# An adaLN block with a spectral filter and a SwiGLU FFN: the order of its loads, its statistics and its inverse transform is changed

## The chip, the cores and the metric

The kernel runs on one core of one Trainium2 chip. The metric is the device time of one execution in microseconds (us). A NeuronCore has five engines that run beside each other and wait for one another through semaphores: TensorE (matmuls; the profile calls it PE, and its weight loads PEld), VectorE (DVE), ScalarE (ACT), GpSimd (POOL) and SyncE (SP, which here only issues DMAs). Each engine works through its own list of instructions in order. Matmuls write to PSUM, a small memory from which only VectorE and ScalarE read here; everything else lies in SBUF, whose first dimension is 128 partitions.

## What is computed

```python
sa, ca, ga, sb, cb, gb = split(silu(c) @ w_mod, 6)          # c: (1, 640), w_mod: (640, 3840)
h = layernorm(x) * (1 + ca) + sa                            # x: (1, 2048, 640)
y = irfft2(rfft2(h) * (w_r + 1j * w_i))                     # over both axes, weights (2048, 321)
x = x + ga * y
h = layernorm(x) * (1 + cb) + sb
g = silu(h @ w_gate)                                        # (640, 1728)
u = h @ w_up
out = x + gb * ((g * u) @ w_down)                           # (1728, 640)
```

Inputs and output are bf16. `rfft2` and `irfft2` are the real two-dimensional Fourier transform over tokens and features and its inverse.

## The kernel before

All work is done with matmuls against constant tables. The 2048 tokens are 16 tiles of 128, `x_sb[:, t]` (token 16 p + t is on partition p). The code is one long list of calls; the order of the calls in the text is the order in each engine's list, since the scheduling is manual. Dependences between tiles become semaphore waits. A tile pool hands out its buffers by tag; a new tile of a tag waits until the old one in that buffer is read. Loads from HBM are DMAs that SP issues in the order of the text (lines 190 to 220 and a few later ones); two of them, the second half of `Wa`, are issued by ScalarE from within its own list (step `W0`, line 206).

**First stage, LN1 and the first transform over tokens (lines 265 to 358).** Per tile t: `ln1_stats` (L269 to L271, VectorE: two `bn_stats` and an aggregate) or, for the tiles in `ON_ACT`, `ln1_act` on ScalarE (a sum, then a sum of squares); `means` (L285, L288) writes the negated mean; `root` (L247, L323, ScalarE) the square root; `ready` takes the reciprocal (L328, VectorE) and calls `scaled`, which multiplies a 128x128 table with 1/std (`Fs`, L295, GpSimd for most tiles, VectorE for the first and last); `turn` (L303, L306, TensorE) multiplies the tile with `Fs` into a PSUM tile `tp`; `turned` (L312, ScalarE, VectorE for the last two) copies it to `hT`. `mod_ca` computes the column form of 1 + ca: 25 small matmuls (L239, into `mpsA`), then an addition on VectorE (`one_p_ca`, L341). `rs` multiplies it into the table `Rp` (L334). The string `plan` (L354) writes out by hand the order in which all these steps are issued: a letter for the step, a number for the tile. In it `a0`, the whole of `mod_ca`, stands after `t5` and before `s9`.

**Second stage, the filter (lines 379 to 508).** The frequencies along the tokens are in 16 groups g. Per group, in the order `order` = 1..10, 0, 11..15: `dfwd` (L383) transforms along the features into `zps`; `zcopy` (L393, ScalarE); `over_t` (L413 to L429) finishes the token transform into `xps`; `xcopy` (L434); `product` (L441, VectorE) multiplies with the weights; `sums` (L448 to L461, VectorE); `over_t_back` (L470 to L474, TensorE), three groups later, into `vps`; `vcopy` (L477, ScalarE) into `V2`. A group has 128 frequencies, one per partition. In `_freqs` (L45) they stand in two halves: slot 0 (32 j + g) on partitions 0 to 63, slot 1 (32 j + 32 - g) on partitions 64 to 127. The weights lie likewise: `Wa` holds groups 0 to 7 and `Wb` groups 8 to 15, and each is loaded in halves of 64 partitions, `slot0` (L202) and `slot1` (L206; rows in reverse, 642 bytes each). `swap(h)` exchanges two columns of a weight tile on VectorE.

**The last products back (lines 515 to 538).** The last four groups' `over_t_back` come after all other work of the filter. Between them stand `gate_rows` for ga (L253, 10 matmuls into `ga_ps`), `mod_cols` for cb and sb (L239, 50 small matmuls into `c_ps`) with two ScalarE operations that read them (L527, L528), two blocks of `keep_warm` (L260, 8 matmuls of constants each), and the DMAs of the gate and down weights `Wg` and `Wd_sb` (L530, L531). `Wg` goes into the buffer of `wm_g`, which the `c_ps` matmuls read. Then VectorE multiplies ga into the table `Rinv_sb` (L536).

**Head of LN2 (lines 641 to 665).** `dinv(t)` (L621, 6 matmuls, then a ScalarE copy `W2`, L624) transforms back along the features; `over_p(t)` (L630, 2 matmuls) finishes the token transform, and VectorE adds the result to `x_sb` in place (L636), or ScalarE copies it and `add_y` adds it (L633, L639) for tiles in `BY_ACT`. Seven `dinv` and four `over_p` run here. For tiles 0 and 1 follow `ln2_stats` (L551 to L553), the root on ScalarE, `ln2_xn` (L578: (x - mean) / std on VectorE into `xn2`), a transpose on TensorE (L591, `tp`) and the affine 1 + cb, sb (L599 VectorE, L601 ScalarE) into `h2Ta`.

**FFN (lines 671 to 735).** The tokens go in five chunks of 2, 4, 4, 4 and 2 tiles (`CHUNKS`); sc is the chunk. Per chunk: `gu13` (L678, the last 64 columns of gate and up together), then 13 rounds fc: ten matmuls into `gu` (L701), silu on ScalarE (`sg`, L704), the product on VectorE into `AT` (L705). Then per tile two halves of 14 down matmuls (L732, `oo`), the addition of x (L734) and the store (L735). Beside the rounds of a chunk VectorE prepares the next one: `ln2_stats` in rounds 1 to 4, `ln2_newton` (L560 to L569, round 5: 1/std by three Newton steps from an integer guess, all on VectorE), `ln2_xn` in rounds 6 and 7, then a DMA transpose (L582) and the affine (L607, L610). L707 multiplies the last 64 columns in round 2.

In chunk 0 more is done. `gate_rows` for gb (L253, `gb_ps`) comes after `gu13`; ten of the 14 row blocks of `Wd_sb` are multiplied with it on GpSimd (L692, the "folds"), the other four on VectorE (L711) in rounds 8 to 11. And round fc runs `over_p(4 + fc)` and `dinv(7 + fc)` ahead of its matmuls, so that all 16 tiles are added to x by round 11. In PSUM `dinv`, `over_p` and the down matmuls share one tag `oo` with two buffers; `gu`, `gu13`, `tp` and the first four `over_p` share `vv` with two.

Of the kernel before, what the change touches and what calls it, by code (L numbers as in the profile page):

```python
# [17 lines left out]
NT, P = 16, 128  # L18
# [106 lines left out]
def adaln_block_kernel(  # L125
# [82 lines left out]
    slot0(0)
    for i in range(2):
        nc.sync.dma_start(Ws[0][64:128, i, 0], w_rows[i][1][:, 0])  # L210
    nc.sync.dma_start(wm_sa[:], wm_v[:, :, 0:D])
    nc.sync.dma_start(Mf[:, 4:8], M_dram[:, 4:8])
    nc.sync.dma_start(Mi[:, 0:8], Mi_dram[:, 0:8])
    slot0(1)
    slot1(nc.sync, 1)
    nc.sync.dma_start(Mf[:, 8:16], M_dram[:, 8:16])
# [45 lines left out]
    with tc.tile_pool(name="ph2", bufs=2) as ph2, \  # L262
# [46 lines left out]
        def turned(t):  # L309
            tp = tps.pop(t)  # L310
            copy = nc.vector.tensor_copy if t >= NT - 2 else nc.scalar.copy
            copy(hT[:, :, :, t, :], tp[:, 0:NC5, :].rearrange("p c (g j) -> p c g j", j=8))  # L312
# [22 lines left out]

        ON_ACT = (1, 8)

        def mod_ca():
            mps = ps1.tile([P, NC5], F32, name="mpsA", tag="xps", bufs=1)
            mod_cols(mps, wm_ca, 0, True)  # L340
            nc.vector.tensor_scalar_add(one_p_ca[:], mps[:], 1.0)  # L341

# [7 lines left out]
            "g": lambda t: nc.gpsimd.tensor_copy(sc_rep[:], sc_col[:].unsqueeze(2).to_broadcast([P, NC5, 128])),  # L350
            "W": lambda t: slot1(nc.scalar, t), "a": lambda t: mod_ca(), "x": lambda t: rs(3 * t, 3 * t + 1, 3 * t + 2),
# [84 lines left out]
        def product(g, PP):  # L436

            X = Xs.pop(g)
            for h in range(2):
                w = Ws[g // 8][:, :, g % 8, 0:LH] if h == 0 else Ws[g // 8][:, :, g % 8, 320:320 - LH:-1]  # L440
                nc.vector.tensor_tensor(PP[:, :, :, LH * h:LH * h + LH], X[:, :, LH * h:LH * h + LH].unsqueeze(1).to_broadcast([P, 2, 2, LH]),  # L441
                                        w.unsqueeze(2).to_broadcast([P, 2, 2, LH]), ALU.mult)
# [72 lines left out]
        for n in range(NGR - 1 - LAG, NGR):  # L515
            if n == 14:
                c_ps = ps1.tile([P, 2, 512], F32, name="c_ps", tag="xps", bufs=1)
                for j, w_ in enumerate((wm_g[:, :, D:2 * D], wm_sb)):
                    mod_cols(c_ps[:, j, 0:NC5], w_, 0)
# [6 lines left out]
            if n == 14:  # L526
                nc.scalar.add(one_p_cb[:], c_ps[:, 0, 0:NC5], 1.0)  # L527
                nc.scalar.copy(modcols[:, 2, :], c_ps[:, 1, 0:NC5])  # L528
                Wg = big.tile([P, NC5, FFM], BF16, name="Wg", tag="wg")
                nc.sync.dma_start(Wg[:], B_w_gate[:, 0:FFM].rearrange("(c5 dp) f -> dp c5 f", dp=P))  # L530
                nc.sync.dma_start(Wd_sb[:, 0:13, :], B_w_down[0:FFM, :].rearrange("(fc fp) d -> fp fc d", fp=P))  # L531
                nc.gpsimd.memset(Wd_sb[64:128, 13, :], 0.0)
                nc.sync.dma_start(Wd_sb[0:64, 13, :], B_w_down[FFM:FF, :])
                keep_warm(ps1, "xps", 1, 8)
# [3 lines left out]
        keep_warm(ps1, "xps", 1, 8)  # L538

# [77 lines left out]
    def dinv(t):  # L617
        o = ps3.tile([P, 2, 512], F32, name="oo", tag="oo")
        for odd, blocks in enumerate(((0, 3, 4), (2, 1, 4))):
# [6 lines left out]
    def over_p(t, tag="vv"):  # L626
        W2 = W2s.pop(t)
        y = ps3.tile([P, 2, 512], F32, name="yy", tag=tag)
        for odd in range(2):
# [10 lines left out]

    BY_ACT = (1, 2, 3)
    ybs = {}
    dinv(0)
    dinv(1)
    over_p(0)
    ln2_stats(0)
    dinv(2)
    over_p(1)
    add_y(1)
# [5 lines left out]
    ln2_xn(0, 1)  # L655
    over_p(2)
    dinv(4)
    dinv(5)
    tp = ln2_turn_pe()
    add_y(2)  # L660
    dinv(6)
    nc.scalar.activation(warm[:], rstd2[:, 1:2], ACT.Silu)
    ln2_affine_pe(tp)
    over_p(3)
    add_y(3)
    AT2 = [big.tile([P, NFC, 512], BF16, name=n, tag=g) for n, g in (("ATa", "w"), ("ATb", "mi"))]
# [4 lines left out]
    for sc, (c0, c1) in enumerate(CHUNKS):  # L671
# [14 lines left out]
        if sc == 0:  # L686

            gb_ps = ps3.tile([P, 2, 512], F32, name="gb_ps", tag="oo")
            gate_rows(gb_ps, wm_gb, False)
            nc.scalar.copy(g_bc[1][:].rearrange("p (o h) -> p o h", o=2), gb_ps[:, :, 0:320])  # L690
            for f in range(10):
                nc.gpsimd.tensor_tensor(Wd_sb[:, f, :], Wd_sb[:, f, :], g_bc[1][:], ALU.mult)  # L692
        for fc in range(NFC - 1):
            if sc == 0 and fc < 12:
                over_p(4 + fc, "oo")
            if sc == 0 and fc < 9:
                dinv(7 + fc)
            gu = ps3.tile([P, 2, 512], F32, name="gu", tag="vv")
# [6 lines left out]
            nc.vector.tensor_tensor(AT[:, fc, :C], gu[:, 1, :C], sg[:, :C], ALU.mult)  # L705
            if fc == 2:
                nc.vector.tensor_tensor(AT[0:64, 13, :C], u13b[:, :C], sg13[:, :C], ALU.mult)  # L707
# [4 lines left out]
            if sc + 1 < len(CHUNKS):  # L712
                m0, m1 = CHUNKS[sc + 1]
                if 1 <= fc < 1 + m1 - m0:
                    ln2_stats(m0 + fc - 1)
                if fc == 5:
                    ln2_newton(sc + 1)
                if fc in (6, 7):
                    for t in range(m0 + 2 * (fc - 6), min(m1, m0 + 2 * (fc - 6) + 2)):
                        ln2_xn(sc + 1, t)  # L720
                if fc == 7:
                    ln2_turn(sc + 1)
        if sc + 1 < len(CHUNKS):
            ln2_affine(sc + 1, range(NC5))
        for tl in range(n):
# [3 lines left out]
            for h in range(2):  # L729
                oo = ps3.tile([P, 2, 512], F32, name="oo", tag="oo")  # L730
                for fc in range(NFC):
# [52 lines left out]
```

## Time and profile before

| | us |
|---|---|
| three runs: median (lowest to highest) | 286.33 (285.9 to 286.36) |
| the profiled execution | 286.61 |
| its span, first to last instruction | 284.8 |
| TensorE busy (share of the span) | 263.7 (93%) |
| VectorE busy | 157.1 (55%) |
| ScalarE busy | 110.6 (39%) |
| GpSimd busy | 28.7 (10%) |
| HBM read and written | 21.53 and 2.62 MB |

The profile is that of one execution. It has a page with totals, and views that answer questions: the chain of work that ended last (followed back from the last instruction, at each step to what released it), busy time in stretches of the span, waits (who stood still for whom: total, times, longest), groups of instructions by source line, and a timeline. In a group, `xN` is the count and the durations are those of one instruction; a matmul's duration includes its way through the array, so dense matmuls overlap, and the time of a run of matmuls is read from the chain or the timeline. `PEclk` is the clock granted to TensorE as a share of the full one. The column DMA is the mean busy share of the 16 DMA engines.

### The profile page before, as it was taken

The numbers are of one execution on the slowest core, as the hardware profiler recorded it, in microseconds if no ns is written. First come the engines' busy times: TensorE is split into PE (matmuls) and PEld (weight loads), VectorE is DVE, ScalarE is ACT, GpSimd is POOL, SyncE is SP. The second block draws the span as 40 slices with busy tenths as digits, with TensorE's granted clock in tenths as the row PEclk, the third lists the DMA queues.
The fourth block names the chain that finished last, engine by engine and source line by source line (L and its number), as shares of the span: only waits on it lengthen the run. The fifth ranks groups of instructions, "written<-read, shape, count | busy, mean of one in ns | idle before, by whom it ended". The sixth has DMA issues, their size and how long they took to land.

```text
span 284.8 us, 4821 instructions
## 1 busy us (share of the span) xinstructions
PE 263.7 (93%) x1926; PEld 174.0 (61%) x1926; DVE 157.1 (55%) x440; ACT 110.6 (39%) x198; POOL 28.7 (10%) x47
## 2 busy tenths in 40 slices
PE   5767999999858988999999999999999999999995
PEld 4555787787635766864445764444774444678873
DVE  4678499789251888924863323883421762422432
ACT  7655787785575434412223003322203222202320
POOL 5552000010003960000000000000000000000000
PEclk9979999999997999999999999999999999999999
DMA  6999999005991000410031011004011002011001
GB/s 221 395 223 348 208 382 323 2 2 165 370 371 38 0 2 1 92 48 10 0 59 37 23 48 32 0 5 90 23 46 35 0 0 46 3 47 53 0 2 46
DMA packets 24905, 27.02 MB, mean 95 GB/s; under 512 B 11313, under 2 KB 21938, under 8 KB 24754
## 3 DMA queue, kind: packets, MB, share of 16 engines
q1 hardware_dynamic: 23808, 26.07, 29.9%
q10 hardware_dynamic: 1074, 0.64, 1.3%
q8 instruction: 15, 0.25, 0.4%
q14 instruction: 8, 0.07, 0.1%
HBM read 21.53 MB, written 2.62 MB: 85 GB/s over the span
## 4 chain that ended last, share of the span: by engine, by line
PE 83%; DVE 9%; ACT 3%; DMA 1%; issue 1%; POOL 0%; SPq 0%; DVEq 0%; ACTq 0%; POOLq 0%
PE gu L701 38%; PE oo L732 21%; PE zps L383 4%; PE oo L621 3%; PE xps L424 2%; PE xps L429 2%; PE tp L303 2%; PE tp L306 2%; PE gu L678 2%; DMA x_sb<-in_A_x_dram 1%; DVE x_sb L636 1%; PE vps L470 1%; PE vps L471 1%; PE gb_ps L253 1%; DVE st L270 1%
## 5 line engine op out<-in xcount | busy, mean ns | idle before, releaser
L704 ACT ACTIVATE sg<-gu 128x512 f32<-128x512 f32 (+1 forms) x65 | 33.2, 511 | 75.3 <-PE gu L701 71.2
L701 PEld LDWEIGHTS <-Wg 128*128 128x128 bf16 x325 | 31.7, 98 | 25.5 <-issue 0.7
L701 PEld LDWEIGHTS <-Wu 128*128 128x128 bf16 x325 | 31.8, 98 | 24.5
L734 DVE TENSOR_TENSOR xo<-oo,x_sb 128x320 bf16<-128x320 f32 x32 | 15.7, 491 | 38.6 <-PE oo L732 38.5
L701 PE MATMUL gu<-h2Ta,Wu 128*128 128x256 bf16 (+1 forms) x195 | 34.6, 308 | 0.0
L701 PE MATMUL gu<-h2Ta,Wg 128*128 128x256 bf16 (+1 forms) x195 | 34.6, 308 | 0.0
L705 DVE TENSOR_TENSOR ATa<-gu,sg 128x256 bf16<-128x256 f32 (+1 forms) x39 | 19.9, 509 | 26.5 <-ACT sg L704 26.4
L705 DVE TENSOR_TENSOR ATb<-gu,sg 128x512 bf16<-128x512 f32 x26 | 17.9, 687 | 28.6 <-ACT sg L704 28.5
L701 PE MATMUL gu<-h2Tb,Wu 128*128 128x512 bf16 x130 | 32.3, 379 | 0.0
L701 PE MATMUL gu<-h2Tb,Wg 128*128 128x512 bf16 x130 | 32.3, 379 | 0.0
L732 PE MATMUL oo<-Wd_sb,ATa 128*128 128x320 bf16 x224 | 30.9, 299 | 0.0
L732 PE MATMUL oo<-Wd_sb,ATb 128*128 128x320 bf16 x224 | 30.8, 299 | 0.0
L732 PEld LDWEIGHTS <-ATb 128*128 128x128 bf16 x224 | 21.8, 98 | 8.9
L732 PEld LDWEIGHTS <-ATa 128*128 128x128 bf16 x224 | 21.9, 98 | 8.6
L681 ACT ACTIVATE sg<-gu 64x512 f32<-64x512 f32 (+1 forms) x5 | 2.5, 505 | 49.8 <-PE gu L678 49.7
L621 PE MATMUL oo<-Rinv_sb,V 128*128 128x320 bf16 x96 | 15.4, 299 | 3.3 <-DVE x_sb L636 2.7
L383 PE MATMUL zps<-Rs,hT 128*128 128x324 bf16 x96 | 15.9, 300 | 0.9 <-DVE wtmp L371 0.9
L624 ACT CAST W<-oo 128x640 bf16<-128x640 f32 x16 | 11.0, 694 | 12.6 <-PE oo L621 12.6
L636 DVE TENSOR_TENSOR x_sb<-yy,x_sb 128x640 bf16<-128x640 f32 x13 | 11.1, 854 | 8.1 <-PE yy L630 8.1
L692 POOL TENSOR_TENSOR Wd_sb<-Wd_sb,gb_bc 128x640 bf16<-128x640 bf16 x10 | 13.8, 1415 | 16.8 <-ACT gb_bc L690 16.8
L303 PE MATMUL tp<-Fs,mh 128*128 128x512 bf16 (+1 forms) x32 | 9.5, 391 | 5.5 <-POOL Fs L295 3.9
L621 PEld LDWEIGHTS <-V 128*128 128x128 bf16 x96 | 9.3, 98 | 8.1 <-issue 4.0
(140 smaller groups left out, 333.1 us busy)
## 6 DMA issues: line engine op xcount, KB each, us to landing
out_dram<-xo SPq DMA_DIRECT2D x16, 160.0 KB, 1.8
Wu<-in_B_w_up_dram SPq DMA_DIRECT2D x1, 2080.0 KB, 9.5
Wg<-in_B_w_gate_dram SPq DMA_DIRECT2D x1, 2080.0 KB, 12.6
Wd_sb<-in_B_w_down_dram SPq DMA_DIRECT2D x1, 2080.0 KB, 17.8
wm_g<-in_w_mod_dram SPq DMA_DIRECT2D x2, 800.0 KB, 15.0
Mi<-tab_Mi SPq DMA_DIRECT2D x2, 768.0 KB, 11.6
x_sb<-in_A_x_dram SPq DMA_DIRECT2D x2, 640.0 KB, 9.2
Mf<-tab_M SPq DMA_DIRECT2D x2, 512.0 KB, 9.9
```

Source lines behind the costliest of these rows:

```text
L303: nc.tensor.matmul(tp[:, lo:lo + n, :], lhsT=mh.to_broadcast([P, 128]), rhs=Fs[:].unsqueeze(1).to_broadcast([P, n, 128]), start=True, stop ...
L306: nc.tensor.matmul(tp[:, c5, :], lhsT=block(x_sb[:, t, :], c5), rhs=Fs[:], start=False, stop=(c5 >= 3))
L383: nc.tensor.matmul(zss[g][:, r, :L], lhsT=hT[:, 2 * r + i, g, :, :].rearrange("p t j -> p (t j)"), rhs=Rs[:, 3 * r + i, :], start=(i == 0) ...
L621: nc.tensor.matmul(o[:, odd, 0:320], lhsT=V2[:, b, t, :, :].rearrange("p g j -> p (g j)"), rhs=Rinv_sb[:, odd, i, :], start=(i == 0), stop ...
L624: nc.scalar.copy(W2s[t][:], o[:, :, 0:320])
L636: nc.vector.tensor_tensor(x1t, y[:, :, 0:320], x1t, ALU.add)
L692: nc.gpsimd.tensor_tensor(Wd_sb[:, f, :], Wd_sb[:, f, :], g_bc[1][:], ALU.mult)
L701: nc.tensor.matmul(gu[:, j, :C], lhsT=w_[:, c5, fc * 128:(fc + 1) * 128], rhs=h2T[:, 0:n, c5, :], start=(c5 == 0), stop=(c5 == NC5 - 1))
L704: nc.scalar.activation(sg[:, :C], gu[:, 0, :C], ACT.Silu)
L705: nc.vector.tensor_tensor(AT[:, fc, :C], gu[:, 1, :C], sg[:, :C], ALU.mult)
L732: nc.tensor.matmul(oo[:, 0, 0:320], lhsT=AT[:, fc, tok], rhs=Wd_sb[:, fc, h * 320:(h + 1) * 320], start=(fc == 0), stop=(fc == NFC - 1))
L734: nc.vector.tensor_tensor(xo[:, h * 320:(h + 1) * 320], oo[:, 0, 0:320], x1[:, t, h * 320:(h + 1) * 320], ALU.add)
```

## The change

There are five groups of edits.

1. **Frequency slots.** The two slots of a group alternate over the partitions (slot 0 on even, slot 1 on odd ones) instead of taking a half each; the tables follow from `_freqs`. `Wa` now holds groups 1 to 8, `Wb` groups 9 to 15 and 0. All weight loads are issued by SP, each to every second partition; there are four more small ones, for group 0. `Mf[4:8]` is issued ahead of `wm_sa`.
2. **Scale weights read later.** `mod_ca` is split: `a0`, the matmuls, stands after `R11`, and `a1`, the addition, after `r13`. The plan is otherwise reordered at its start (tile 1 on VectorE, tile 2 on ScalarE), and only the last `turned` is on VectorE.
3. **Products back without stops.** The last four `over_t_back` and `vcopy` follow each other with only `gate_rows` for ga between. Only the `mod_cols` of cb follow, then the DMAs of `Wg` and `Wd_sb`. Both `keep_warm` blocks are gone. `mod_cols` of sb and `gate_rows` of gb move to the head of LN2, ahead of the transpose of tiles 0 and 1.
4. **Newton on GpSimd.** The guess stays on VectorE (three instructions), a product with -0.5 and the three steps, four instructions each, go to GpSimd, one round earlier. Of the ten folds on GpSimd four stay at the start of chunk 0, six follow the Newton steps in round 4. L707's product in chunk 0 moves from round 2 to round 10.
5. **Six tiles of x in the second chunk.** The head of LN2 runs `dinv(0)` to `dinv(4)` and `over_p(0)`, `over_p(1)`; chunk 0 runs `over_p(2)` to `over_p(9)` and `dinv(5)` to `dinv(9)`; `dinv(10)` to `dinv(15)` run in even rounds and `over_p(10)` to `over_p(15)` in odd rounds of chunk 1. The silu table load of ScalarE comes after the affine and `dinv(4)`. `oo` becomes two tags of one buffer each: `ob` for `dinv` from tile 4 on, `oa` for `over_p` in the FFN; the down matmuls alternate between them.

```diff
-    k = np.zeros((NGR, 2, 64), dtype=np.int64)
+    k = np.zeros((NGR, 64, 2), dtype=np.int64)
...
-        k[g, 0] = 32 * np.arange(64) + g
-        k[g, 1] = 32 * np.arange(64) + (32 - g if g else 16)
+        k[g, :, 0] = 32 * np.arange(64) + g
+        k[g, :, 1] = 32 * np.arange(64) + (32 - g if g else 16)
...
+    def filter_rows(h):
+        n = 8 - h
+        for i in range(2):
+            nc.sync.dma_start(Ws[h][1::2, i, 0:n], w_rows[i][1][:, 15 - 8 * h:(7 if h == 0 else 0):-1])
+        for i in range(2):
+            nc.sync.dma_start(Ws[h][0::2, i, 0:n], w_rows[i][0][:, 1 + 8 * h:1 + 8 * h + n])
+        if h == 1:
+            for s_ in range(2):
+                for i in range(2):
+                    nc.sync.dma_start(Ws[1][s_::2, i, 7], w_rows[i][s_][:, 0])
...
-        ON_ACT = (1, 8)
+        ON_ACT = (2, 8)
...
+        def mod_ca(step):
+            if step == 0:
+                mps.append(ps1.tile([P, NC5], F32, name="mpsA", tag="xps", bufs=1))
+                mod_cols(mps[0], wm_ca, 0, True)
+            else:
+                nc.vector.tensor_scalar_add(one_p_ca[:], mps[0][:], 1.0)
...
-        plan = """s0 m0 r0 c0 g0 s2 p1 q1 m1 r1 y0 t0 s3 M2 R2 s4 y1 e0 t1 Y2 s5 M4 R4 p8 W0 e1 t2 t3 s6 Y4 e2 s7 M6 R6
-                  e3 q8 m8 r8 t4 t5 a0 s9 Y6 e4 s10 M9 R9 e5 t6 t7 s11 y8 Y9 e6 e7 t8 s12 M11 R11 e8 t9 s13 m13 r13 t10 Y11
-                  e9 e10 t11 s14 m14 r14 y13 t12 e11 s15 m15 r15 e12 t13 y14 e13 t14 x0 y15 t15 e14 x1 k8 e15"""
+        plan = """s0 m0 r0 c0 g0 s1 m1 r1 y0 t0 p2 q2 m2 r2 s3 m3 r3 y1 t1 e0 s4 y2 y3 t2 e1 s5 M4 R4 s6 t3 e2 Y4 p8 s7
+                  M6 R6 e3 t4 t5 q8 m8 r8 s9 Y6 e4 s10 M9 R9 e5 t6 t7 s11 y8 Y9 e6 e7 t8 s12 M11 R11 a0 e8 t9 s13 m13 r13
+                  a1 t10 Y11 e9 e10 t11 s14 m14 r14 y13 t12 e11 s15 m15 r15 e12 t13 y14 e13 t14 x0 y15 t15 e14 x1 k8
+                  e15"""
...
+        hv = ph4.tile([P, n], F32, name="rs_hv")
+        nc.gpsimd.tensor_scalar_mul(hv[:], v[:], -0.5)
...
-            nc.vector.tensor_tensor(tt[:], y, y, ALU.mult)
-            nc.vector.scalar_tensor_tensor(tt[:], tt[:], -0.5, v[:], ALU.mult, ALU.mult)
-            nc.vector.scalar_tensor_tensor(rstd2[:, g] if it == 2 else y, tt[:], 1.5, y, ALU.add, ALU.mult)
+            nc.gpsimd.tensor_tensor(tt[:], y, y, ALU.mult)
+            nc.gpsimd.tensor_tensor(tt[:], tt[:], hv[:], ALU.mult)
+            nc.gpsimd.tensor_scalar_add(tt[:], tt[:], 1.5)
+            nc.gpsimd.tensor_tensor(rstd2[:, g] if it == 2 else y, tt[:], y, ALU.mult)
...
-            for f in range(10):
+            for f in range(4):
                 nc.gpsimd.tensor_tensor(Wd_sb[:, f, :], Wd_sb[:, f, :], g_bc[1][:], ALU.mult)
...
-            if sc == 0 and fc < 12:
-                over_p(4 + fc, "oo")
-            if sc == 0 and fc < 9:
-                dinv(7 + fc)
+            if sc == 0 and fc < 8:
+                over_p(2 + fc, "oa")
+            if sc == 0 and fc < 5:
+                dinv(5 + fc)
+            if sc == 1 and fc % 2 == 0 and fc < 12:
+                dinv(10 + fc // 2)
+            if sc == 1 and fc % 2 == 1 and fc < 12:
+                over_p(10 + fc // 2, "oa")
...
-            if fc == 2:
+            if fc == (10 if sc == 0 else 2):
                 nc.vector.tensor_tensor(AT[0:64, 13, :C], u13b[:, :C], sg13[:, :C], ALU.mult)
...
-                if fc == 5:
+                if fc == m1 - m0:
                     ln2_newton(sc + 1)
+                    for f in range(4, 10) if sc == 0 else ():
+                        nc.gpsimd.tensor_tensor(Wd_sb[:, f, :], Wd_sb[:, f, :], g_bc[1][:], ALU.mult)
```

More of the change, by code (lines that the diff above doesn't have):

```diff
@@ L334, in rs @@
                 nc.vector.tensor_scalar_mul(Rs[:, i, :], Rp[:, i, :], one_p_ca[:, (i if i < 3 else i - 1):(i if i < 3 else i - 1) + 1])
-        ON_ACT = (1, 8)
[L338 to L341, printed above, removed]
+        ON_ACT = (2, 8)
+        mps = []
+        def mod_ca(step):
[4 more added lines that the diff above has]
+                nc.vector.tensor_scalar_add(one_p_ca[:], mps[0][:], 1.0)
         steps = {
@@ L515, in adaln_block_kernel @@
         for n in range(NGR - 1 - LAG, NGR):
[L516 to L519, printed above, removed]
             over_t_back(order[n], ("vps", "zps")[n % 2])
@@ L525, in adaln_block_kernel @@
                 nc.scalar.copy(g_bc[0][:].rearrange("p (o h) -> p o h", o=2), ga_ps[:, :, 0:320])
[L526 to L534, printed above, removed]
+        c_ps = ps1.tile([P, 2, 512], F32, name="c_ps", tag="xps", bufs=1)
+        mod_cols(c_ps[:, 0, 0:NC5], wm_g[:, :, D:2 * D], 0)
+        Wg = big.tile([P, NC5, FFM], BF16, name="Wg", tag="wg")
+        nc.sync.dma_start(Wg[:], B_w_gate[:, 0:FFM].rearrange("(c5 dp) f -> dp c5 f", dp=P))
+        nc.sync.dma_start(Wd_sb[:, 0:13, :], B_w_down[0:FFM, :].rearrange("(fc fp) d -> fp fc d", fp=P))
+        nc.gpsimd.memset(Wd_sb[64:128, 13, :], 0.0)
+        nc.sync.dma_start(Wd_sb[0:64, 13, :], B_w_down[FFM:FF, :])
+        nc.scalar.add(one_p_cb[:], c_ps[:, 0, 0:NC5], 1.0)
         for odd in range(2):
@@ L627, in over_p @@
         W2 = W2s.pop(t)
-        y = ps3.tile([P, 2, 512], F32, name="yy", tag=tag)
+        y = ps3.tile([P, 2, 512], F32, name="yy", tag=tag, bufs=2 if tag == "vv" else 1)
         for odd in range(2):
@@ L639, in add_y @@
         nc.vector.tensor_tensor(x1[:, t, :], ybs.pop(t)[:], x1[:, t, :], ALU.add)
-    BY_ACT = (1, 2, 3)
+    BY_ACT = (1,)
+    T_IN_FFN = 4
     ybs = {}
@@ L646, in adaln_block_kernel @@
     ln2_stats(0)
+    over_p(1)
     dinv(2)
-    over_p(1)
     add_y(1)
@@ L655, in adaln_block_kernel @@
     ln2_xn(0, 1)
-    over_p(2)
+    c_ps = ps3.tile([P, 2, 512], F32, name="c_ps", tag="oa", bufs=1)
+    mod_cols(c_ps[:, 0, 0:NC5], wm_sb, 0)
+    nc.scalar.copy(modcols[:, 2, :], c_ps[:, 0, 0:NC5])
+    gb_ps = ps3.tile([P, 2, 512], F32, name="gb_ps", tag="ob", bufs=1)
+    gate_rows(gb_ps, wm_gb, False)
+    tp = ln2_turn_pe()
+    nc.scalar.copy(g_bc[1][:].rearrange("p (o h) -> p o h", o=2), gb_ps[:, :, 0:320])
+    ln2_affine_pe(tp)
     dinv(4)
[L658 to L661, printed above, removed]
     nc.scalar.activation(warm[:], rstd2[:, 1:2], ACT.Silu)
-    ln2_affine_pe(tp)
-    over_p(3)
-    add_y(3)
     AT2 = [big.tile([P, NFC, 512], BF16, name=n, tag=g) for n, g in (("ATa", "w"), ("ATb", "mi"))]
@@ L729, in adaln_block_kernel @@
             for h in range(2):
-                oo = ps3.tile([P, 2, 512], F32, name="oo", tag="oo")
+                oo = ps3.tile([P, 2, 512], F32, name="oo", tag=("oa", "ob")[h], bufs=1)
                 for fc in range(NFC):
```

26 lines of the change are left out of this document (8 added, 18 removed).

## The prediction

> **What bounds the kernel now.** I read the chain of work that ended last first, then a table of busy time by stage, then the waits. The chain's shares by engine, and some of its pieces (start us, us, what):
>
> ```profile
> PE 83%; DVE 9%; ACT 3%; DMA 1%; issue 1%; POOL 0%; SPq 0%; DVEq 0%; ACTq 0%; POOLq 0%
> ```
>
> ```profile
> 14.95 0.62 PE mpsA L239 x25
> ...
> 83.62 1.28 ACT L662
> 85.12 0.92 ACT h2Ta L601 x2
> 86.08 0.80 PE gu L678 x5
> 86.87 2.68 PE gb_ps L253 x10
> ...
> 126.99 28.17 PE gu L701 x130
> 155.16 15.21 PE oo L732 x112
> ```
>
> TensorE carries the end. From 118.31 us on it is dense: 130 gate/up matmuls are one piece of 28.17, 112 down matmuls one of 15.21. What is taken off other engines there is worth nothing, and what is added to TensorE there costs its full time. The stages that I use (span cut at first `zps`, first `oo` of `dinv`, first `gu13`, first down matmul):
>
> ```profile
> 0.00:27.86 27.86, 18.96 (x178) 14.50 (x179) 18.79 (x72) 17.64 (x38) 13.28 (x34) 0.94 0.97 298
> 27.86:73.79 45.93, 44.03 (x477) 35.38 (x478) 35.44 (x119) 33.11 (x52) 1.61 (x3) 1.00 0.63 193
> 73.79:86.08 12.29, 8.05 (x61) 5.37 (x61) 5.97 (x15) 8.74 (x15) 0.00 (x0) 1.00 1.05 361
> 86.08:118.31 32.23, 29.31 (x225) 22.55 (x225) 23.84 (x57) 12.97 (x25) 13.76 (x10) 0.95 0.12 24
> 118.31:284.80 166.49, 163.32 (x988) 96.24 (x986) 73.09 (x179) 38.09 (x69) 0.00 (x0) 1.00 0.11 28
> ```
>
> Columns: stretch, its length, busy time of TensorE, its weight loads, VectorE, ScalarE, GpSimd, clock, DMA share, GB/s. TensorE has idle time to win in rows 1, 3 and 4 (8.9, 4.2, 2.9 us), hardly any in row 5.
>
> **Part 1, first stage (LN1).** One wait stands out:
>
> ```profile
> DVE one_p_ca L341 <- PE mpsA L239: 3.8, 1, 3.8
> ```
>
> VectorE stands at `one_p_ca` from 11.83 to 15.60, because `a0` waits for matmuls that are queued behind `t5`. The statistics of tile 9 start only after it, and TensorE idles 15.57 to 17.65. With `a` split, the matmuls come after `t8` and the add after `s13`, so the wait goes. Laying the new plan out by its rows (a tile's statistics 1.05, `turned` on ScalarE 0.65 back to back, a GpSimd `Fs` 0.60, a turn on TensorE 1.07 slow or 0.55 fast), statistics of tile 9 start at 12.0 and the VectorE list ends with `e15` at 23.8. What is late next is ScalarE: 15 `turned` (9.8), two tiles of sums and squares (3.6), 13 roots (about 3), early idle of 2 to 3, from 4.7 on: it also ends at 23.8. Its two L206 DMA issues (0.69 and 0.68) go to SP. So `zps` could start at 24.0 instead of 27.86. TensorE at its slow rate until 21 us would give 25.2, slow throughout 26.7. I take 3.0, between 0.5 (the other queues fill the hole) and 3.8.
>
> **Part 2, loads.** Same bytes. Two rows show the weight loads, two others not (columns as above):
>
> ```profile
> 14.80:21.70 6.90, 4.52 (x54) 3.37 (x52) 5.93 (x22) 3.55 (x8) 3.99 (x9) 0.75 1.10 216
> 21.70:28.50 6.80, 5.12 (x58) 3.64 (x57) 5.66 (x23) 3.60 (x8) 1.35 (x3) 1.00 1.06 353
> 28.50:35.30 6.80, 6.80 (x63) 4.94 (x62) 2.91 (x8) 4.85 (x7) 0.00 (x0) 1.00 1.11 200
> 35.30:42.00 6.70, 6.70 (x87) 5.51 (x83) 6.60 (x23) 5.41 (x9) 0.00 (x0) 1.00 1.05 380
> ```
>
> With `Wa` and then `Wb` in flight the engines are full, yet move 200 to 216 GB/s instead of 353 to 380. The last `Wa` landed by 24.2 (issued 10.6, 13.6 to landing); its first product ran at 31.69, about 28.7 after part 1. So 4.5 us hide it, and I count 0. The four extra small issues (about 0.47 each on SP) delay `Mf[8:16]` by 2 from about 38.8; it is first used near 46, or 43 after part 1: hidden. Bounds: nothing, and rival (d).
>
> **Part 3, products back.** After the last `xps` TensorE now runs c_ps (50 matmuls), two `keep_warm` blocks (0.61 each) and waits for ScalarE (0.91). Without them, the last `over_t_back` waits for its sums on VectorE, ready at 69.8; it takes 0.7, its `vcopy` 0.70 after 0.25 latency: 71.55. `dinv(0)` starts at 71.6 instead of 73.79: 2.2 gained. The Rinv product (69.8 to 71.0) is done by then. `Wg` is issued at 71.2 instead of 69.66, behind `Wu`'s 2 MB, so I leave its landing at 82.3; its first use is near 82.6.
>
> **Part 4, head of LN2 (12.29 now).** Times from here in the old clock of that stage. `over_p(1)` before `dinv(2)` moves little: VectorE ends the statistics of tile 1 at 80.04 (was 80.14), `tp` at 81.1 to 81.9. New on TensorE before it: 25 c_ps matmuls (0.6) and `gate_rows` (1.25 at full clock), both in TensorE's wait for `xn2`. ScalarE's two affines no longer stand behind `dinv(6)`'s copy and the 1.28 table load: 82.05 to 83.05. `gu13` starts at 83.15: 2.9 gained. `gb_ps`'s slow 2.68 is inside the next stage's gain.
>
> **Part 5, first chunk (32.23 now).** TensorE's work is 0.55 + 5 x 0.82 + 8 x 0.27 + 13 x 1.09 = 21.0. ScalarE's table load now stands ahead of `sg13`, so the first product `AT` is at 87.0. From there VectorE's round (add 0.80, product 0.34, statistics 1.04 = 2.18) equals TensorE's (0.27 + 0.82 + 1.09 = 2.18); `over_p` in its one buffer waits for the add before (0.6, 0.6 and 1.4 us idle). The variances are ready at 97.95 and VectorE reaches the `xn2` of tile 2 at 101.5. Newton now is 13 GpSimd instructions, each dependent. They are bounded by 0.16 (the same on VectorE, L567) and 1.40 (a fold, L692); I take 0.25, since L288 with 128x2 elements takes 0.227 and the fold has 160 times the elements: end 101.6. Folds 0 to 3 are done before (the DMA wait of L692 ends at 88.0, in this clock 90.2, then 4 x 1.40). Folds 4 to 9 start at 101.6 and need six times 1.36 to 1.40, and the down matmuls wait for them. Beside them VectorE has nine instructions that read and write SBUF alone: four `xn2`, four folds, L707. The one row of that kind:
>
> ```profile
> L707 DVE TENSOR_TENSOR ATa<-u13b,sg x3: 406/673/1309, 97.5 to 263.9; 64x256 bf16<-64x256 bf16 x2, 64x512 bf16<-64x512 bf16 x1
> ```
>
> ```profile
> L692 POOL TENSOR_TENSOR Wd_sb<-Wd_sb,gb_bc x10: 1393/1397/1574, 90.4 to 102.8; 128x640 bf16<-128x640 bf16 x10
> ```
>
> (ns min/median/max.) The 256-column form takes 406 alone and 1309 in the middle of the folds, and one fold became 1574: it waited for the fold's end. The adds from PSUM (0.82 to 0.88) show no such wait. The price per instruction thus lies between 0 and about 0.9; I take L707's for all nine, `xn2` too, as none touches PSUM. Laid out in turn, `xn2` of tile 5 ends at 109 (or 106 if a pair stays together), VectorE's products are late, TensorE waits 0.7 to 3.4 us before each of `gu` 9 to 12, and the down matmuls start effectively at 112.7 to 114.2: the stage takes 29.5 to 31.0. I take 30.2: 2.0 gained, though 5.7 us of matmuls left it (four tiles' `dinv` and `over_p`, `gate_rows`). The Trainium skill (SBUF — State Buffer, Who interferes with whom) says that a VectorE instruction with two SBUF inputs, or in a two-port mode as `tensor_scalar` may be, blocks against a GpSimd one that reads SBUF, for the whole instruction. By that rule the `xn2` wait as I took them; L707 agrees for the first kind, no row shows the second; by the rule the sum is the one below, without it that of rival (a).
>
> **Part 6, second chunk.** Six `dinv` (0.82) and six `over_p` (0.27) come into a stage that TensorE fills: 6.6 lost. Per two rounds (5.4 on TensorE) VectorE has about 4.4 and ScalarE 1.9, so nothing stalls. Newton on GpSimd is hidden in this and the later chunks (two rounds of 2.17).
>
> **Sum.** -3.0 - 2.2 - 2.9 - 2.0 + 6.6 = -3.5. The profiled execution took 286.61 (span 284.8, 1.8 around it): 283.1. The median shown is 0.28 lower: **282.8**. Its own range, from part 1 (1.2 to 3.8) and part 5 (1.2 to 2.7): 281.3 to 285.4, chance 0.55.
>
> **Rivals.** (a) The `xn2` don't wait for GpSimd, only the folds and L707 do. For it: no row shows a `tensor_scalar` waiting. Then `xn2` of tile 5 ends at 104.4, the stage takes 27.8: 280.4. Chance 0.15. (b) Part 1 gives 0.5: ScalarE, with its list as long as VectorE's, or slow matmuls fill the hole. For it: matmuls of `tp` ran at 0.53 per five until 21.5. 285.3, chance 0.10, half of it within 0.2%. (c) Slower: GpSimd's chain becomes the bound of chunk 0. Every us by which Newton ends later moves `xn2`, folds 4 to 9 and the down matmuls by one. 13 x 0.52 = 6.8 instead of 3.25 uses up the 3.5; from there it is slower: at 0.60 each 287.4, at the fold's 1.40 some 298. For it: the queue is in order and dependent, and a two-input form this small is in no row. Against: 0.227 at L288. Chance 0.16. (d) The change doesn't do what it says in the loads: one queue, or every second partition, makes `Wa` twice as slow (6.9 more): it lands at 31.1, 2.4 after its use: 285.2. Against: the transfers keep their pieces, and 4.5 us hide them. Chance 0.04. The Trainium skill (SBUF — State Buffer, Door 1: The DMA port swizzle) says that partitions 0 to 63 reach only half of the 16 ports; by that rule every second partition reaches all, the loads get faster and this rival falls. The 200 and 216 GB/s agree with the slow half.
>
> Faster by over 0.2% (about what a measurement here can tell): 0.53 + 0.15 + 0.05 + 0.02 = 0.75; within: 0.02 + 0.05 + 0.01 = 0.08; slower 0.17. The range 279.5 to 287.0 leaves out most of (c) and the low end of (a).
>
> **What would show it.** Part 1: no VectorE wait at `one_p_ca`, first `zps` at 24 to 26. Part 3: first `dinv` 43.7 to 43.8 after it. Part 4: `gu13` 9.4 later, no slow clock after it. Part 5: `xn2` rows of 1 us and more, some of 0.44; Newton steps on GpSimd near 0.25; first down matmul 29 to 31 after `gu13`. Part 6: the second chunk 6.6 longer, dense. A gap of TensorE in the second chunk, or weights that land after the first product, would prove me wrong.

## The result, and the profile after

| | us |
|---|---|
| before, median of 4 runs (lowest to highest) | 286.15 (285.9 to 286.36) |
| after, median of 4 runs | 281.56 (281.45 to 283.38) |
| ratio, 95% interval | 0.9855, 0.9814 to 0.9896 |
| after, the profiled execution and its span | 281.63, 279.5 |

The kernel is 1.4% faster by the ratio, 4.6 us between medians, where the prediction had 3.5. The stages of the changed kernel, cut at the same four instructions as before and at the `gu13` of chunk 2 (columns as in the prediction):

```profile
0.00:23.59 23.59, 17.98 (x179) 13.64 (x179) 18.28 (x71) 18.12 (x40) 13.60 (x35) 1.00 0.94 330
23.59:66.84 43.25, 42.34 (x437) 33.94 (x438) 35.52 (x120) 32.89 (x51) 1.61 (x3) 1.00 0.56 192
66.84:75.41 8.57, 7.98 (x79) 5.46 (x80) 4.93 (x13) 4.61 (x8) 0.00 (x0) 1.00 1.06 376
75.41:106.57 31.16, 24.45 (x185) 18.48 (x183) 24.00 (x46) 11.68 (x24) 16.85 (x23) 0.95 0.36 97
106.57:165.04 58.47, 58.47 (x352) 34.27 (x351) 27.74 (x58) 16.39 (x26) 2.69 (x13) 1.00 0.11 28
165.04:279.50 114.46, 111.13 (x686) 66.66 (x683) 45.72 (x99) 25.97 (x49) 5.33 (x26) 1.00 0.10 27
```

The lengths are to be compared row by row: 27.86 became 23.59 (-4.3), 45.93 became 43.25 (-2.7), 12.29 became 8.57 (-3.7), 32.23 became 31.16 (-1.1). The fifth row, 58.47, stood at 52.06 before (118.31 to 170.37): +6.4, and TensorE is busy in all of it. The last row is the same as before within 0.03. The sum is -5.3, that of the spans.

The fourth row is the odd one. The inverse transform of four tiles (six went to the second chunk, two came in from the head) and the rows of the gate gb left that stage, and it got hardly shorter; TensorE's idle time there grew from 2.9 to 6.7 us. The timeline of the changed kernel shows VectorE (start us, us, engine, line, operation):

```profile
95.93 2.92 DVE L582 TENSOR_SCALAR xn2c<-x_sb,mv,rstd 128x640 bf16<-128x640 bf16 x2 [0.28 <-POOL rstd L573]
...
99.86 1.87 DVE L582 TENSOR_SCALAR xn2c<-x_sb,mv,rstd 128x640 bf16<-128x640 bf16 x2
...
103.58 1.34 DVE L717 TENSOR_TENSOR Wd_sb<-Wd_sb,gb_bc 128x640 bf16<-128x640 bf16 x1
...
105.52 0.48 DVE L717 TENSOR_TENSOR Wd_sb<-Wd_sb,gb_bc 128x640 bf16<-128x640 bf16 x1
```

and GpSimd at the same time:

```profile
95.69 0.20 POOL L573 TENSOR_TENSOR rstd<-rs_t,rs_yi 128x4 f32<-128x4 f32 x1
95.84 8.73 POOL L725 TENSOR_TENSOR Wd_sb<-Wd_sb,gb_bc 128x640 bf16<-128x640 bf16 x6
```

From 95.84 to 104.57 GpSimd folds. In that time two `xn2` take 2.92 us and the next two 1.87, a VectorE fold 1.34. As soon as GpSimd is done, a fold of the same size takes 0.48. From 95.93 to 105.27 the chain of work that ended last runs through VectorE alone.

### The profile page after: what moved, and what is told of

The parts are those of the page before. It is cut to its first block, busy times and chain, and to the rows that moved or that the text cites. A ratio compares the mean times of both kernels' runs of the same rounds, so it can differ in the third digit from the quotient of the medians.

```text
span 279.5 us, 4802 instructions
## 1 busy us (share of the span) xinstructions
PE 262.4 (94%) x1910; PEld 172.4 (62%) x1910; DVE 156.2 (56%) x404; ACT 109.7 (39%) x198; POOL 40.1 (14%) x100
## 4 chain that ended last, share of the span: by engine, by line
PE 78%; DVE 11%; ACT 4%; DMA 2%; issue 1%; POOL 1%; SPq 1%; ACTq 0%; DVEq 0%; POOLq 0%
PE gu L707 36%; PE oo L740 22%; PE zps L389 4%; PE oo L625 3%; PE xps L430 2%; PE xps L435 2%; DMA x_sb<-in_A_x_dram 2%; DVE xn2c L582 2%; PE gu L683 1%; DVE st L271 1%; DVE st L270 1%; ACT W L628 1%; DVE ATa L711 1%; DVE Wd_sb L717 1%; PE yy L634 1%
## 5 line engine op out<-in xcount | busy, mean ns | idle before, releaser
L707 PEld LDWEIGHTS <-Wg 128*128 128x128 bf16 x325 | 32.1, 99 | 27.1 <-issue 3.6
L707 PEld LDWEIGHTS <-Wu 128*128 128x128 bf16 x325 | 32.1, 99 | 24.8
L707 PE MATMUL gu<-h2Ta,Wg 128*128 128x256 bf16 (+1 forms) x195 | 35.5, 315 | 3.1 <-DVE ATa L711 3.1
L711 DVE TENSOR_TENSOR ATa<-gu,sg 128x256 bf16<-128x256 f32 (+1 forms) x39 | 19.9, 510 | 27.8 <-ACT sg L710 27.8
L707 PE MATMUL gu<-h2Ta,Wu 128*128 128x256 bf16 (+1 forms) x195 | 35.2, 312 | 0.0
L707 PE MATMUL gu<-h2Tb,Wu 128*128 128x512 bf16 x130 | 32.3, 379 | 0.0
L707 PE MATMUL gu<-h2Tb,Wg 128*128 128x512 bf16 x130 | 32.3, 379 | 0.0
L567 POOL TENSOR_SCALAR rs_hv<-veps 128x4 f32<-128x4 f32 (+1 forms) x4 | 0.9, 229 | 111.0 <-DVE veps L561 111.0
L389 PE MATMUL zps<-Rs,hT 128*128 128x324 bf16 x96 | 15.9, 301 | 0.5 <-DVE hT L313 0.5
L640 DVE TENSOR_TENSOR x_sb<-yy,x_sb 128x640 bf16<-128x640 f32 x15 | 12.8, 854 | 4.6 <-PE yy L634 4.6
L440 ACT CAST X<-xps 128x648 bf16<-128x648 f32 x16 | 11.2, 698 | 6.2 <-PE xps L435 4.5
L628 ACT CAST W<-oo 128x640 bf16<-128x640 f32 x16 | 11.1, 692 | 6.0 <-PE oo L625 5.9
L399 ACT CAST Z<-zps 128x648 bf16<-128x648 f32 x16 | 11.2, 698 | 4.7 <-PE zps L389 2.5
## 6 DMA issues: line engine op xcount, KB each, us to landing
Wg<-in_B_w_gate_dram SPq DMA_DIRECT2D x1, 2080.0 KB, 11.1
```

Of the source, the lines that this page charges most:

```text
L389: nc.tensor.matmul(zss[g][:, r, :L], lhsT=hT[:, 2 * r + i, g, :, :].rearrange("p t j -> p (t j)"), rhs=Rs[:, 3 * r + i, :], start=(i == 0) ...
L399: nc.scalar.copy(Z, z[:, :, :L])
L440: nc.scalar.copy(Xs[g][:], xpss.pop(g)[:, :, :L])
L628: nc.scalar.copy(W2s[t][:], o[:, :, 0:320])
L640: nc.vector.tensor_tensor(x1t, y[:, :, 0:320], x1t, ALU.add)
L707: nc.tensor.matmul(gu[:, j, :C], lhsT=w_[:, c5, fc * 128:(fc + 1) * 128], rhs=h2T[:, 0:n, c5, :], start=(c5 == 0), stop=(c5 == NC5 - 1))
```

## The experiments

Each is an edit of the changed kernel. "First zps" and so on are the cuts of the table above; times are medians, and ratios are to runs of the kernel before on the same chip.

### Part 1: the split, the order, the loads

**a_together**: both steps of the scale weights at the old place.

```diff
-  ... t4 t5 q8 m8 r8 s9 ... R11 a0 e8 ... r13 a1 t10
+  ... t4 t5 a0 a1 q8 m8 r8 s9 ... R11 e8 ... r13 t10
```

> The changed kernel with the products of the scale weights and VectorE's read of them together again behind the turns of tiles 4 and 5. Theory (the late read made the gain of part 1): VectorE waits again at the read of one_p_ca, 2 to 4 us; the first zps comes at 25.5 to 27.5 us instead of 23.59, and the time is 283.5 to 285.5. Rival (the gain came from the full-rate loads and the freed ScalarE queue): the wait is hidden, the first zps stays under 24.3, the time at 281.3 to 282.3.

284.77 us, ratio 0.9966 (0.9934 to 0.9998). First `zps` at 25.5, as the theory says: +1.9. (The profiled span is 2.6 us longer; most of the rest lies in the first chunk, with the same code there.) VectorE stands still for just that long:

```profile
DVE one_p_ca L346 <- PE mpsA L240: 1.9, 1, 1.9
```

**old_plan**: the whole `plan` of before (without its load step), `ON_ACT` and the copies by VectorE.

> The changed kernel with before's whole order of LN1 (statistics of tile 1 on ScalarE, the two steps of the scale weights together, the last two copies out of PSUM on VectorE), loads and the rest as changed. Putting the two steps together alone cost 1.9 us at the first zps (23.6 to 25.5). Theory (the other 2.4 us of part 1 come from the reordered statistics): first zps at 27.0 to 28.2 us, time 285.2 to 286.8. Rival (they come from ScalarE not issuing loads): first zps at 25.0 to 26.0, time 283.0 to 284.8.

286.49 us, ratio 1.0023 (1.0003 to 1.0043): all that the change gains is gone. First `zps` at 27.8, against 27.86 before, with the new loads in place. The wait is 3.4 us here:

```profile
DVE one_p_ca L346 <- PE mpsA L240: 3.4, 1, 3.4
```

So the first stage's 4.2 us are the order of the steps: taken back in this sequence, 1.9 by the split and 2.3 by the reordering around it. 1.5 of the 2.3 show as the same wait being shorter (1.9 instead of 3.4); the rest I did not take apart.

**old_loads**: the halves of 64 partitions, two loads issued by ScalarE (`W0` after `p8`), `Mf[4:8]` behind `wm_sa` again, everything else as changed.

```diff
-    k = np.zeros((NGR, 64, 2), dtype=np.int64)
+    k = np.zeros((NGR, 2, 64), dtype=np.int64)
...
-            "a": mod_ca,
+            "W": lambda t: slot1(nc.scalar, t), "a": mod_ca,
...
```

> The changed kernel with the whole load scheme of before: frequency slots in halves of 64 partitions, two of the loads issued by ScalarE. Theory (the loads are covered; part 2 is worth nothing): 200 to 220 GB/s in the stretches that load W instead of 340 to 406, the loads end some 7 us later, yet the first zps stays within 0.5 us of 23.59 and the time within 0.8 us of 281.56. Rival (part 2 gives the 1.3 us by which part 1 was better than forecast): first zps at 24.6 to 25.2, time 282.6 to 283.2, or more if a W arrives too late for the first product.

281.91 us, ratio 0.9864 (0.9827 to 0.9900), not to be told from the changed kernel's; first `zps` at 23.2. The loads did change. From 10 us on, this kernel and then the changed one (last column GB/s):

```profile
10.00:23.00 13.00, 9.31 (x124) 6.80 (x121) 11.61 (x46) 10.97 (x24) 6.88 (x15) 1.00 1.08 288
```

```profile
10.00:23.60 13.60, 11.60 (x132) 8.59 (x130) 12.22 (x48) 11.15 (x25) 7.11 (x16) 1.00 1.06 389
```

A third more bytes per second, and the time is the same.

### Part 3: the products back

**old_back**: the block of before, with both modulation products, their two reads on ScalarE, the DMAs of `Wg` and `Wd_sb` and the `keep_warm` blocks, between the last products.

> The changed kernel with before's block at the end of the products back (both modulation products and their two ScalarE reads between the products of group 14, the keep-warm matmuls), the rest as changed. Theory: the stretch from the first zps to the first dinv is 45.4 to 46.1 us again instead of 43.25; the head after it is up to 0.6 us shorter, since one product is gone from there; time 283.2 to 284.4. Rival (the stops were not it, the loads of before slowed that stretch): 43.2 to 43.8 us, time 281.2 to 282.2.

285.26 us, ratio 0.9985 (0.9956 to 1.0014). The stage is back at before's length:

```profile
23.70:69.60 45.90, 44.01 (x478) 35.37 (x478) 35.49 (x119) 33.11 (x52) 1.61 (x3) 1.00 0.58 202
```

That is 2.65 more than 43.25, as the theory has it. The head did not get shorter for the product that left it (8.60): that product ran there in TensorE's wait for `xn2`, as the prediction had it. The median is 1 us above the expected range; the profiled span (282.7) shows 3.2 of the 3.7 us, of which 0.5 lie in the first chunk.

### Parts 4 and 5: the folds, the Newton steps and the six tiles

**no_late_folds**: the six late folds are left out, so six row blocks of the down weights lack their gate.

> The changed kernel without its six late GpSimd folds: six row blocks of the down weights are not multiplied by the gate, the rest is the same. Theory: xn2 at about 0.44 us each and every VectorE fold at 0.48, the first chunk 2.5 to 4.5 us shorter, the time 277 to 279. Rival (not the folds): xn2 stays above 0.9 us, the time at 281.3 to 282.

277.51 us, ratio 0.9707 (0.9677 to 0.9736). First chunk:

```profile
75.40:102.30 26.90, 22.67 (x184) 17.65 (x183) 19.14 (x46) 11.68 (x24) 8.17 (x17) 1.00 0.37 101
```

26.90 instead of 31.16, and VectorE is busy for 4.9 us less, though not one of its instructions left. Up to 95.9 us the two chunks are alike. From there to the first down matmul it is 10.67 us with the late folds and 6.40 without; VectorE is busy for 10.64 and 5.75 of them, with 15 instructions each time. The theory stands: the late folds cost 4.3 us of the chunk, through VectorE.

**newton_back**: the Newton steps on VectorE in before's three-operation form, but in the change's round 4; all ten folds start when `Wd` lands.

```diff
-            for f in range(4):
+            for f in range(10):
...
-            nc.gpsimd.tensor_tensor(tt[:], y, y, ALU.mult)
...
+            nc.vector.tensor_tensor(tt[:], y, y, ALU.mult)
+            nc.vector.scalar_tensor_tensor(tt[:], tt[:], -0.5, v[:], ALU.mult, ALU.mult)
+            nc.vector.scalar_tensor_tensor(rstd2[:, g] if it == 2 else y, tt[:], 1.5, y, ALU.add, ALU.mult)
...
```

> The changed kernel with the Newton steps of LN2 on VectorE again and all ten GpSimd folds in one run from the landing of Wd. Theory (the late folds make the four xn2 and the first VectorE folds long): the folds end near 97.5, so at least the last two xn2 and all VectorE folds run alone at about 0.44 and 0.48 us, and the first two at most as long as now; the first down matmul comes 1.5 to 3.0 us earlier after the first gu13, the time is 278.5 to 280.2. Rival (their length has another cause, or VectorE's own Newton steps eat the gain): the time is 281.3 to 283.

288.38 us, ratio 1.0083 (1.0056 to 1.0109): slower than before. Both the theory and the rival missed. GpSimd folds from 84.23 to 97.78, and VectorE meets it with other instructions than I thought of:

```profile
92.45 1.31 DVE L563 TENSOR_SCALAR rs_yi<-veps 128x4 int32<-128x4 int32 x1
...
95.15 1.31 DVE L568 TENSOR_TENSOR rs_t<-rs_yi 128x4 f32<-128x4 f32 x1
96.49 1.31 DVE L569 SCALAR_TENSOR_TENSOR rs_t<-rs_t,veps 128x4 f32<-128x4 f32 x1
97.84 0.16 DVE L570 SCALAR_TENSOR_TENSOR rs_yi<-rs_t,rs_yi 128x4 f32<-128x4 f32 x1
```

Four elements per partition take 1.31 us beside the folds and 0.16 after them. The instructions of 1.31 us each came when the next fold had just begun, so they cost about one fold's length, whatever their size. TensorE meanwhile waits 8.0 us for a sum into x that stands behind these steps, and then runs at a lower clock (columns as above):

```profile
92.00:99.00 7.00, 0.04 (x1) 0.00 (x0) 6.64 (x11) 0.38 (x1) 5.78 (x5) 0.85 0.00 0
99.00:105.00 6.00, 4.99 (x29) 3.57 (x29) 3.83 (x8) 0.66 (x2) 0.00 (x0) 0.61 0.00 0
```

Busy 0.04 us of 7, then a granted clock of 0.61. That an idle TensorE loses its clock is what the Trainium skill (TensorE: Matmul & The Clock Gate, Part 1) says; the trace agrees. Up to the second chunk's `gu13` this costs 3.5 us over the changed kernel; another 3.7 come in the chunks behind, of which the next runs tell.

**six_early**: six folds on GpSimd before the Newton steps, none after; VectorE does the other eight in rounds 8 to 12. The same products at other places.

```diff
-            for f in range(4):
+            for f in range(6):
...
-    folds = {8: (10,), 9: (11,), 10: (12,), 11: (13,)}
+    folds = {8: (6,), 9: (7,), 10: (8, 9), 11: (10, 11), 12: (12, 13)}
...
-                    for f in range(4, 10) if sc == 0 else ():
-                        nc.gpsimd.tensor_tensor(Wd_sb[:, f, :], Wd_sb[:, f, :], g_bc[1][:], ALU.mult)
```

> The changed kernel with six GpSimd folds before the Newton steps and none after; the other eight are done by VectorE in rounds 8 to 12. The same products, other places. Theory (VectorE's instructions that read and write SBUF alone wait for GpSimd's folds, and only then are folds dear): xn2 at 0.44 and each VectorE fold at 0.48 us, the first chunk 2.8 to 4.2 us shorter than the changed kernel's, time 277.4 to 279.0. Rival (eight folds and the last rounds are too much for VectorE): first chunk at most 1.5 us shorter, time 280 to 282.

278.27 us, ratio 0.9735 (0.9716 to 0.9753): 3.3 us faster than the changed kernel, and 7.7 than before by the medians on its chip (285.92). VectorE did four folds more and is done sooner:

```profile
96.09 0.80 DVE L582 TENSOR_SCALAR xn2c<-x_sb,mv,rstd 128x640 bf16<-128x640 bf16 x2 [0.29 <-POOL rstd L573]
...
97.89 0.80 DVE L582 TENSOR_SCALAR xn2c<-x_sb,mv,rstd 128x640 bf16<-128x640 bf16 x2
```

```profile
75.60:102.50 26.90, 22.65 (x183) 17.70 (x182) 19.15 (x46) 11.68 (x24) 10.88 (x19) 1.00 0.39 99
```

Two `xn2` take 0.80 instead of 2.92 and 1.87, and the chunk 26.90, as without the late folds.

**six_early_v**: six_early with the Newton steps on VectorE, as in newton_back.

> The version with six early folds, and the Newton steps on VectorE in before's three-operation form: nine steps at 0.16 us a fifth of a us apart, 1.8 us, where GpSimd's thirteen took 3.8. Theory (with no fold beside them the engine of the Newton steps hardly counts): rstd2 is ready some 1.9 us earlier, VectorE's sums into x1 of that round come 1.8 us later; within 0.7 us of 278.27 either way. Rival (Newton on VectorE is dear by itself, as its run with the ten early folds could suggest at 288.4): 281 or more.

284.1 us, ratio 0.9938 (0.9914 to 0.9963): the rival. The steps are as short as forecast (0.16 each, 92.44 to 94.18, no fold beside them), but in round 4 they stand behind the statistics of the fourth tile and ahead of the next sum into x. TensorE waits 3.3 us for that sum, and the clock of 92 to 100 us is 0.79. Each later chunk, from `gu13` to `gu13`, takes more too: 51.5, 45.7 and 46.2 us against 50.9, 44.4 and 44.4 of six_early. The wait of chunk 2:

```profile
PE gu L704 <- DVE ATa L708: 1.1, 1, 1.1
```

Before, with the same steps on VectorE one round later, the full chunks took 44.5, 44.5 and 44.4. So it looks as if the combination counts: Newton may come a round earlier because it is on GpSimd. VectorE in round 5 of the changed kernel was not tried.

**tiles_in_chunk0**: all sixteen tiles' inverse transform in the first chunk.

```diff
-            if sc == 0 and fc < 8:
+            if sc == 0:
                 over_p(2 + fc, "oa")
-            if sc == 0 and fc < 5:
+            if sc == 0 and fc < 11:
                 dinv(5 + fc)
...
```

> The changed kernel with all sixteen tiles' inverse transform in the first chunk again (rounds 0 to 12 and one behind them), the rest as changed. The second chunk is 6.2 to 6.6 us shorter in every theory. Theory (the first chunk is set by VectorE beside the GpSimd folds, so its idle TensorE time can't take the work): the first chunk is 5 to 6.5 us longer, the time 280.3 to 282.0. Rival (the work hides in the 6.7 us in which TensorE is idle in the first chunk): at most 2 us longer, time 275.0 to 277.3. Other rival (a longer stall and a slow clock behind it): time above 283.

281.37 us, ratio 0.9840 (0.9823 to 0.9856): the changed kernel's time. From the first chunk's `gu13` to the second's it takes 44.9 us instead of 38.6 (+6.3), the second 44.4 instead of 50.9 (-6.5). So the move of six tiles, whose price in the second chunk was the largest term of the prediction's sum, is worth nothing by itself here.

**six_tiles0**: six_early with all sixteen tiles in the first chunk.

> The version with six early folds, and all sixteen tiles' inverse transform in the first chunk. Theory (the move of six tiles is worth nothing as long as the first chunk's rounds have no idle time left to hold them: rounds 8 to 12 are dense at 1.1 us with VectorE's folds in them): first chunk 5 to 7 us longer than the 26.9 us of that version, second 6.4 shorter, time 277.3 to 279.3. Rival (the late folds were what kept the first chunk from holding them): first chunk at most 3.5 us longer, time 274.5 to 276. Other rival: VectorE, with its folds and these sums, is the bound and the slow clock follows: over 280.

281.24 us, ratio 0.9816 (0.9785 to 0.9848): 3.0 us slower than six_early, the third case. In the profiled execution (282.55, at the long end of its 279.99 to 282.55) the first chunk takes 36.1 us, 9.2 more than in six_early, where the theory had 5 to 7. From 103 to 112.2 us VectorE is busy for 7.85 of 9.2 us and TensorE for 5.68: two folds, a sum and a product on VectorE are more than what a round then has for TensorE. Without the late folds the move of six tiles pays.

**best1**: six_early, with all five affines of the first chunk on VectorE.

```diff
-            if c5 < 3:
+            if c5 < 5:
                 nc.vector.tensor_scalar(to, tp[:, c5], ...
```

> The version with six early folds, and all five modulations of the first chunk's transposed tokens on VectorE, where ScalarE's two began only when VectorE's three were done. Theory (ScalarE's two wait for VectorE's three, since they write the same tile, and cost the last two matmuls of gu13 0.7 us): two more on VectorE at about 0.35 us instead of ScalarE's 1.0, the wait gone or halved, 0.2 to 0.6 us less: 277.7 to 278.1. Rival (it is the read of PSUM or the queue of ScalarE, and the next round waits as long for something else): 278.2 to 278.6.

278.69 us, ratio 0.9736 (0.9712 to 0.9759): no gain. The wait in front of `gu13`'s last matmuls is gone, as the theory says, and VectorE comes to Newton's guess 1.2 us sooner after `gu13`, while the sixth fold still runs:

```profile
90.65 1.31 DVE L563 TENSOR_SCALAR rs_yi<-veps 128x4 int32<-128x4 int32 x1
92.00 0.17 DVE L564 TENSOR_SCALAR rs_yi<-rs_yi 128x4 int32<-128x4 int32 x1
```

The gain is given back at this meeting with a fold, whose end is set by the landing of `Wd`. TensorE now waits 2.6 us for the sum behind it (1.3 in six_early), and the clock of 90 to 98 us is 0.79 instead of 1.00: the first down matmul comes 27.8 us after `gu13` instead of 26.8.

**old_head**: tiles 2 and 3 finished and tiles 5 and 6 begun ahead of `gu13` as before; the sb product and the gb gate stay there too.

```diff
+    over_p(2)
+    dinv(4)
+    dinv(5)
     gb_ps = ps3.tile([P, 2, 512], F32, name="gb_ps", tag="ob", bufs=1)
...
+    add_y(2)
+    dinv(6)
     ln2_affine_pe(tp)
-    dinv(4)
+    over_p(3)
+    add_y(3)
...
```

> The changed kernel with tiles 2 and 3 finished and tiles 5 and 6 begun between the first statistics and gu13, as before, and with ScalarE taking the sums of tiles 2 and 3. Theory (the head lost its 3.7 us since this work left it): the head is 2.0 to 3.8 us longer than 8.57; the first chunk, in which VectorE is late beside the folds anyway, 0 to 2 us shorter; time 282 to 285. Rival (the work only changed its place, and the head's time is that of the chain of statistics, xn2 and transposes): head at most 1 us longer, time 280.5 to 282.

286.96 us, ratio 1.0025 (1.0009 to 1.0040), above the theory's range. The head takes 15.9 us (66.7 to 82.6), the first chunk 29.2. VectorE waits 5.4 us for the transposes, which stand behind all of this in TensorE's list, and the granted clock of 74 to 78 us is 0.76. So the direction of the theory holds. The head is longer than before's 12.29, and two things that before did not have there can be seen: the gate's ten matmuls (2.8 us), and waits of 1.3 and 0.8 us for the copy `W2`, since tiles 4 and 5 and the gate share the one buffer of `ob`. So this run does not show the price of the moved work alone.

## Why the prediction came out right, and where it did not

- **Part 1** was mis-sized: -3.0 forecast, -4.3 measured, beyond the bound of 3.8. Of the 1.3 us, 0.9 come from my leaning towards a slow TensorE: the groups of five matmuls in the turns followed each other every 0.53 us only until 14.2 us, then every 0.28 (before: mostly 0.53 until about 21.5). The other 0.4 are the layout at full speed, 24.0, which was too long and was the bound. old_plan and a_together show two contributions of about 2 us each, where I had named one wait. Rival (b), a gain of 0.5, is out.
- **Part 2**, nothing: right (old_loads). Rival (d) is out: the loads came faster, not slower. The Trainium skill (SBUF — State Buffer, Door 1: The DMA port swizzle) has partitions 0 to 63 on half of the ports; 389 against 288 GB/s agree.
- **Part 3**: -2.2 forecast, -2.7 measured; old_back gives 2.65 back. The 0.5 more was not taken apart.
- **Part 4**: the head gave 3.7 instead of 2.9, but one step failed. ScalarE's two affines did not run beside VectorE's three but behind them:

```profile
74.86 1.05 DVE L603 TENSOR_SCALAR h2Ta<-tp,one_p_cb,modcols 128x256 bf16<-128x256 bf16 x3 [0.61 <-ACT gb_bc L667]
...
76.08 1.02 ACT L605 ACTIVATE h2Ta<-tp,modcols,one_p_cb 128x256 bf16<-128x256 bf16 x2 [1.58 <-PE gu L683]
...
80.88 0.42 DVE L711 TENSOR_TENSOR ATa<-gu,sg 128x256 bf16<-128x256 f32 x1 [2.27 <-ACT sg L710]
```

`gu13` could start on VectorE's three, which shortens the head as the stages are divided here, but its last two matmuls waited 0.7 us for ScalarE's two. Counted from the first `dinv`, the first product `AT` came after 14.0 us, where 13.2 were forecast (87.0 less 73.79). Why ScalarE waited stays open: the profile names matmuls of `gu13`, my explanation was the tile that both engines write, and no run separates the two. best1 shows that taking this wait away gains nothing in the end.

- **Part 5**, first chunk: -2.0 forecast, -1.1 measured; with the head -4.8, where -4.9 was forecast. The mechanism was right, and rival (a) is out: `xn2`, a `tensor_scalar` on SBUF alone, does wait for GpSimd's folds. no_late_folds shows the price, 4.3 us. That the number came so near is partly luck: counted from the first `dinv`, Newton's end was 1.2 us later than forecast, and from there to the first down matmul it took 10.7 us instead of 11.1 to 12.6. I took 0.9 us for each of nine instructions; six met a fold, at 0.8 each (4.9 together), and the last three ran after it. What I had wrong is the kind of price. It is the rest of the running fold, for an instruction of 640 elements or of 4, and "reads and writes SBUF alone" is too wide: `bn_stats` does so too and stays at 0.48 beside the folds, as the sums from PSUM stay at 0.82 to 0.88. The Trainium skill (SBUF — State Buffer, Who interferes with whom) has this rule: an exclusive lock for the whole instruction, and no contention for an instruction with at most one SBUF input outside the two-port modes. The trace agrees with both halves.
- **Rival (c)**, GpSimd's Newton chain as the bound: out. 13 instructions of 0.20 to 0.24 us ran from 92.11 to 95.89, 0.29 apart; I took 0.25.
- **Part 6**: +6.6 forecast, +6.4 measured, dense.

The total was right to 1.2 us: parts 1 and 3 gave 1.8 more than forecast, the rest came out even, and 0.3 more time lay around the span (2.1 us instead of 1.8). Small differences in the first chunk say little: in the changed kernel, a_together, old_plan, old_loads and old_back, which have the same code there, it takes 38.6 to 39.3 us from `gu13` to `gu13`.

What I did not see is that the move of the six tiles cancels itself: it takes 6.3 us out of the first chunk and puts 6.5 into the second (tiles_in_chunk0). Nearly the whole gain is the first stage; parts 3 to 6 together give 1.1 us. What the first chunk could have won was spent on waits for the late folds, and six_early, which takes those away, makes it 278.27 us, with best1 (278.69) the fastest here of the kernels that compute all.

## What to carry to other kernels

Before work is given to GpSimd, list which VectorE instructions will run beside it. Here `tensor_scalar` from SBUF to SBUF and instructions with two SBUF inputs waited for the running fold, so each can cost as much as one GpSimd instruction, and a chain of tiny ones is dearest for its work. Lay GpSimd's long instructions where VectorE works from PSUM or on statistics, and give the rest to VectorE: eight folds of 0.48 us on VectorE were cheaper than four there with six more beside it on GpSimd. And when a stage gets lighter without getting shorter, look for what now fills it before the move is credited or blamed.

## What the runs showed of the hardware that I had not expected

- A VectorE instruction on 128x4 elements took 1.31 us beside GpSimd's folds and 0.16 alone, `tensor_scalar` on int32 included.
- Dependent GpSimd instructions on 128x4 elements came every 0.29 us at 0.20 to 0.24 each; the same steps on VectorE every 0.20 at 0.16. So GpSimd is not far behind at this size.
- One VectorE list that is late by 1.8 us in round 4 cost 5.8 us in the whole (six_early_v): 2.9 up to the second chunk's `gu13`, where TensorE waits 3.3 us and the clock behind falls, and the rest in the three chunks behind it, where the place repeats (in chunk 2 a wait of 1.1 us, at a clock of 1.00).
